# Moving the final output store of a decode kernel from SyncE to ScalarE

## The chip, the cores and the metric

The kernel runs on one core of a Trainium2 chip. The metric is the device time of one execution in microseconds (us). "Time" below is always that figure. "Span" is what the trace covers, from the first to the last recorded instruction; it is somewhat shorter than the time.

Names: PE is the matrix engine, DVE the vector engine, ACT or ScalarE the activation engine, POOL or GpSimd the general one, SP or SyncE the engine that here only synchronises and issues transfers. "SPq" and "ACTq" are the instruction sequencers of SyncE and ScalarE. A semaphore is a counter on which an engine can wait; a transfer increments one as it completes, and its landing is the last of these increments. DVE's last operation converts the result to bf16 in the tile `fin_bf`; it is called the cast below.

## The reference

One decode step: layer norm of a single row, attention of 32 query heads over 8 K/V heads with 65,536 cached positions each, an output projection, and a small feed-forward network in parallel.

```python
xn = _layernorm(x)                               # x is [1, 1, 512]
# attention: q = xn @ wq; k_cache, v_cache are [1, 8, 65536, 128] in bf16
o  = softmax(q k^T / sqrt(128)) v                # 32 heads, 4 per K/V head
return x + o @ wo + (gelu(xn @ w1 + b1) @ w2 + b2)   # [1, 1, 512], bf16
```

The two caches are 134 MB each, so the step is mostly a matter of reading about 280 MB once. The output is 512 bf16 numbers, 1 KB.

## The kernel before

A small scheduler in the program records operations for each engine with what they read and write, and derives the semaphore waits. SyncE issues every large load. The operations before the last few are emitted in a block, at whose end all engines meet at a barrier; the rest is emitted after it. This is the end of the program, the only part that the change touches:

```python
    rest = {}
    for i, (g0, n) in enumerate(WP):
        if i == 1:                                   # from here on: after the block
            rest.update((e, len(e.ops)) for e in (PE, DVE, SP))
        for r in range(g0 * HPG, (g0 + n) * HPG):
            for kt in range(KT):
                fin_mm(kt, oX_bf[:, r:r + 1], wo_sb[:, r, kt * 128:(kt + 1) * 128], ...)
    ...                                              # the last head's matmuls
    NR = 32 * (KT - 1) + 1
    sch.op(DVE, lambda: dve.tensor_copy(out=fin_bf[0:NR, :], in_=pR[0:NR, 0:128]),
           reads=[f"pss{R}"], writes=["fin"])
    ev_out = sch.dma(
        SP,
        lambda: sp.dma_start(out=out[0, 0].rearrange("(kt p) -> kt p", p=128), in_=fin_bf[0:NR:32, :]),
        sem_out, reads=["fin"], writes=["out_dram"],
    )
    ...
    with nc.Block() as block:
        ...                                          # gpsimd: _emit(e, POOL.ops)
        @block.sync
        def _(e):
            _emit(e, SP.ops[:rest[SP]])
        @block.scalar
        def _(e):
            _emit_rolled(e, ACT.ops, [m[1] for m in marks2])
        ...                                          # vector, tensor
    for e, obj in ((PE, pe), (DVE, dve), (SP, sp)):
        _emit(obj, e.ops[rest[e]:])
    sp.wait_ge(ev_out.sem, ev_out.val)
```

The four parts of the result stand in partitions 0, 32, 64 and 96, so the store moves four rows of 256 bytes.

## Time and profile before

| | before |
|---|---|
| time, median of 3 runs | 656.82 us (656.76 to 657.03) |
| span of the profiled run | 655.5 us |
| last weight rows landed, by the chain of waits | 652.7 us |
| end of the cast of the result, `fin_bf` | 653.79 us |
| last instruction (SyncE, landing of the store) | 655.49 us |

First, lines of the page of the profiled run of before: the span; the busy share of the DMA engines in 40 equal slices, in tenths (9 is 90% or more); two of the DMA queues with their packets, megabytes and share of the 16 engines' time; the HBM traffic; and the chain of work that ended last, by engine.

```profile
span 655.5 us, 27968 instructions
...
DMA  9999999999999999999999999999999999999997
...
q1 hardware_dynamic: 8616, 280.50, 99.4%
...
q10 hardware_dynamic: 148, 0.01, 0.0%
...
HBM read 280.50 MB, written 0.00 MB: 428 GB/s over the span
...
DMA 63%; PE 34%; issue 2%; DVE 0%; SPq 0%
```

The DMA engines are busy for 90% or more of all slices but the last (70%), and the chain lies in DMA and PE: the kernel is a stream of loads with PE close behind it. Queue 1 is SyncE's; queue 10 is ScalarE's, with 148 packets from three small loads at the start.

The timeline of before near its end has, per row, start and duration in us, engine, line of the kernel, operation, output and input, and in brackets the idle time before it with what ended it:

```profile
652.82 0.36 PEld L805 LDWEIGHTS pss<-kv,oT_all 128*1 128x1 bf16 x16 [0.76 <-issue]
652.85 0.60 PE L805 MATMUL pss<-kv,oT_all 128*1 128x128 bf16 x16 [0.50 <-DMA kv<-in_A_wo_dram]
653.50 0.29 DVE L823 CAST fin_bf<-pss 97x128 bf16<-97x128 f32 x1 [4.78 <-PE pss L805]
653.82 0.64 SPq L827 DMA_DIRECT2D out_dram<-fin_bf  x1
```

And the waits of SyncE in before: waiter, what it waited for, total us, times, longest.

```profile
SPq L842 <- PEq L842: 13.8, 1, 13.8
...
SPq L827 <- DVE fin_bf L823: 3.4, 1, 3.4
SPq L866 <- DMA out_dram<-fin_bf: 1.0, 1, 1.0
```

The last load, in the chain of before and then in that of after (start and duration in us):

```profile
635.59 17.13 DMA kv<-in_A_wo_dram
```

SyncE stands at the block's barrier for 13.8 us, then waits 3.4 us for the cast, issues the store, and waits 1.0 us for it to land. The engine that issues the store is never late.

### The profile page before, as it was taken

How to read it: one execution, taken by the hardware profiler on the slowest of the kernel's cores; microseconds unless marked ns; L12 is line 12 of the kernel's file. 1: busy time of each engine (PE TensorE's matmuls, PEld its weight loads, DVE VectorE, ACT ScalarE, POOL GpSimd, SP SyncE). 2: the span in 40 equal slices, each digit the busy share in tenths (PEclk: the TensorE clock that was granted, in tenths of full speed). 3: DMA queues.
4: the chain of work that ended last, by engine and by line, in shares of the span. 5: the costliest groups of instructions: out<-in, count | busy, mean ns of one | idle time of the engine just before them, and what ended most of it. 6: DMA issues, size and time to landing. Idle time of an engine off the chain costs nothing.

```text
span 655.5 us, 27968 instructions
## 1 busy us (share of the span) xinstructions
PE 536.8 (82%) x12682; PEld 509.6 (78%) x12682; DVE 275.8 (42%) x574; ACT 245.0 (37%) x454; POOL 2.9 (0%) x27
## 2 busy tenths in 40 slices
PE   2478699989789697878969788896978879797897
PEld 0277598979788696878959687895978879697886
DVE  3244072625436171453516245261534516154353
ACT  0134162634425162352506235160443516145251
POOL 0000000000000000000000000000000000000000
PEclk9788596967869596786959679595886959578695
DMA  9999999999999999999999999999999999999997
GB/s 386 445 431 422 431 430 432 446 422 450 416 448 420 428 460 404 436 428 454 430 420 440 426 442 422 426 460 408 444 426 450 430 418 436 428 460 404 432 432 305
DMA packets 8774, 280.65 MB, mean 428 GB/s; under 512 B 1082, under 2 KB 1596, under 8 KB 1724
## 3 DMA queue, kind: packets, MB, share of 16 engines
q1 hardware_dynamic: 8616, 280.50, 99.4%
q8 instruction: 8, 0.13, 0.1%
q10 hardware_dynamic: 148, 0.01, 0.0%
q14 instruction: 2, 0.02, 0.0%
HBM read 280.50 MB, written 0.00 MB: 428 GB/s over the span
## 4 chain that ended last, share of the span: by engine, by line
DMA 63%; PE 34%; issue 2%; DVE 0%; SPq 0%
DMA kv<-in_A_k_cache_dram 61%; PE pst L590 27%; PE pss L610 4%; DMA kv<-in_A_wo_dram 3%; PE pO L681 2%; PE pA L637 0%; PE pA L648 0%; DVE pmax L618 0%; PE pA L697 0%; PE pss L805 0%; DVE gmax L639 0%; DVE diag L641 0%; SPq L470 0%; SPq L467 0%; DVE fin_bf L823 0%
## 5 line engine op out<-in xcount | busy, mean ns | idle before, releaser
L600 ACT ACTIVATE kt_ring<-pst 128x1024 bf16<-128x1024 bf16 x192 | 195.6, 1027 | 310.6 <-PE pst L590 309.2
L590 PE MATMUL pst<-ident_bf,kv 128*128 128x128 bf16 x4096 | 281.8, 235 | 34.5 <-DMA kv<-in_A_k_cache_dram 34.4
L590 PEld LDWEIGHTS pst<-ident_bf,kv 128*128 128x128 bf16 x4096 | 263.5, 107 | 42.8 <-DMA kv<-in_A_k_cache_dram 35.9
L598 DVE COPY kt_ring<-pst 128x1024 bf16<-128x1024 bf16 x320 | 210.7, 687 | 119.1 <-PE pst L590 116.9
L681 PE MATMUL pO<-P_bf,kv 128*128 128x4 bf16 x4096 | 115.1, 166 | 37.6 <-DMA kv<-in_A_v_cache_dram 31.2
L681 PEld LDWEIGHTS pO<-P_bf,kv 128*128 128x128 bf16 x4096 | 113.6, 104 | 38.9 <-DMA kv<-in_A_v_cache_dram 32.2
L610 PE MATMUL pss<-q_cur,kt_ring 128*128 128x4 bf16 x4096 | 111.9, 164 | 5.1 <-issue 5.1
L610 PEld LDWEIGHTS pss<-q_cur,kt_ring 128*128 128x128 bf16 x4096 | 109.3, 96 | 5.3 <-issue 5.3
L659 ACT ACTIVATE P_bf<-pss,negm 128x128 bf16<-128x128 f32 x128 | 50.9, 548 | 67.4 <-DVE negm L651 67.4
L690 DVE COPY o_all<-pO 128x4 f32 (+1 forms) x32 | 5.2, 162 | 120.7 <-PE pO L681 119.9
L618 DVE TENSOR_REDUCE pmax<-pss 128x4 f32<-128x512 f32 x32 | 22.1, 692 | 69.0 <-PE pss L610 69.0
L659 ACT ACTIVATION_READ_ACCUMULATOR P_bf<-pss,negm 128x1 f32 x128 | 35.4, 277 | 0.0
L648 PEld LDWEIGHTS pA<-diag,ones_f 4*128 4x128 f32 x64 | 12.6, 244 | 18.1 <-DVE diag L641 16.5
L637 PE MATMUL pA<-ident_f,pmax 128*4 128x128 f32 x64 | 14.2, 310 | 12.6 <-DVE pmax L618 12.6
L648 PE MATMUL pA<-diag,ones_f 4*128 4x4 f32 x64 | 15.4, 309 | 10.0 <-DVE diag L641 10.0
L637 PEld LDWEIGHTS pA<-ident_f,pmax 128*4 128x4 f32 x64 | 2.9, 84 | 15.7 <-DVE pmax L618 14.0
L639 DVE TENSOR_REDUCE gmax<-pA 4x1 f32<-4x128 f32 x32 | 8.8, 274 | 9.4 <-PE pA L637 9.4
L673 DVE COPY sums_all<-sums 128x8 f32 (+1 forms) x16 | 2.7, 172 | 23.4 <-ACT P_bf L659 23.4
L697 PE MATMUL pA<-sums_all,ones_f 128*128 128x128 f32 x32 | 12.4, 491 | 0.0
L518 PE MATMUL pA<-ones_bf,xn_row 1*128 1x1 bf16 x4 | 0.3, 172 | 12.7 <-DVE xn_row L514 12.7
L518 PEld LDWEIGHTS pA<-ones_bf,xn_row 1*128 1x128 bf16 x4 | 0.2, 115 | 12.7 <-DVE xn_row L514 12.7
L651 DVE TENSOR_SCALAR negm<-pA 128x4 f32<-128x4 f32 x32 | 5.1, 161 | 10.8 <-PE pA L648 10.8
(78 smaller groups left out, 63.8 us busy)
## 6 DMA issues: line engine op xcount, KB each, us to landing
kv<-in_A_k_cache_dram SPq DMA_DIRECT2D x32, 4096.0 KB, 27.5
kv<-in_A_v_cache_dram SPq DMA_DIRECT2D x4, 4096.0 KB, 23.1
kv<-in_A_wq_dram SPq DMA_DIRECT2D x1, 4096.0 KB, 12.3
kv<-in_B_w_dram SPq DMA_DIRECT2D x2, 1792.0 KB, 17.8
kv<-in_A_wo_dram SPq DMA_DIRECT2D x1, 2048.0 KB, 23.7
kv<-in_A_wo_dram SPq DMA_DIRECT2D x1, 1024.0 KB, 25.9
kv<-in_A_wo_dram SPq DMA_DIRECT2D x1, 512.0 KB, 26.6
kv<-in_A_wo_dram SPq DMA_DIRECT2D x1, 384.0 KB, 17.1
```

The lines of the kernel that those rows point to most:

```text
L590: lambda tb=tb, at=at, b=b, tt=s * TPB + t: pe.transpose(pst[tb][:, at * 128:(at + 1) * 128], slot[b][:, tt, :], ident_bf[:, :]),
L598: e, fn = DVE, lambda tb=tb, dst=dst: dve.tensor_copy(out=dst, in_=pst[tb][:, :])
L600: e, fn = ACT, lambda tb=tb, dst=dst: act.activation(out=dst, in_=pst[tb][:, :], func=ACTF.Copy)
L610: lambda k=k, kb=kb, at=at, t=t: pe.matmul(pss[k][:, at:at + HPG], lhsT=kt_ring[:, kb * BCOL + t * 128:kb * BCOL + (t + 1) * 128], rhs=q_c ...
L618: lambda k=k: dve.tensor_reduce(out=pmax[:, :], in_=pss[k][:, 0:CW].rearrange("p (t j) -> p j t", j=HPG), axis=AX.X, op=ALU.max),
L637: sch.op(PE, lambda: pe.matmul(pA[0:HPG, PA_ST:PA_ST + 128], lhsT=pmax[:, 0:HPG], rhs=ident_f[:, :], start=True, stop=True), reads=["pmax" ...
L639: sch.op(DVE, lambda: dve.tensor_reduce(out=gmax4[:, :], in_=pA[0:HPG, PA_ST:PA_ST + 128], axis=AX.X, op=ALU.max), reads=["pA"], writes=[" ...
L648: sch.op(PE, lambda: pe.matmul(pA[:, PA_SB:PA_SB + HPG], lhsT=ones_f[0:HPG, 0:128], rhs=diag4[0:HPG, 0:HPG], start=True, stop=True), reads ...
L659: lambda k=k, at=at, j=j, src=src: act.activation(out=P_v[k][:, :, j], in_=src[:, :, j], func=ACTF.Exp, bias=negm[:, at:at + 1], scale=1.0 ...
L681: lambda k=k, t=t: pe.matmul(pO[:, 0:HPG], lhsT=vslot[:, k * TPD + t, :], rhs=P_v[k][:, t, :], start=t == 0, stop=t == TPD - 1),
L690: sch.op(DVE, lambda: dve.tensor_copy(out=o_all[:, at_pair(i, PW, k * HPG, HPG)], in_=pO[:, 0:HPG]), reads=["pO"], writes=[f"o{k}"])
L697: sch.op(PE, lambda: pe.matmul(pA[:, PA_SUM:PA_SUM + NC], lhsT=ones_f[:, :], rhs=sums_all[:, :], start=True, stop=True), reads=["ones_f", ...
```

## The change

The store and the wait for its landing move from SyncE to ScalarE, whose own work has ended by then. SyncE's program then ends at the block's barrier.

```diff
-            rest.update((e, len(e.ops)) for e in (PE, DVE, SP))
+            rest.update((e, len(e.ops)) for e in (PE, DVE, ACT))
...
     ev_out = sch.dma(
-        SP,
-        lambda: sp.dma_start(out=out[0, 0].rearrange("(kt p) -> kt p", p=128), in_=fin_bf[0:NR:32, :]),
+        ACT,
+        lambda: act.dma_start(out=out[0, 0].rearrange("(kt p) -> kt p", p=128), in_=fin_bf[0:NR:32, :]),
         sem_out, reads=["fin"], writes=["out_dram"],
     )
...
-            _emit(e, SP.ops[:rest[SP]])
+            _emit(e, SP.ops)
...
-            _emit_rolled(e, ACT.ops, [m[1] for m in marks2])
+            _emit_rolled(e, ACT.ops[:rest[ACT]], [m[1] for m in marks2])
...
-    for e, obj in ((PE, pe), (DVE, dve), (SP, sp)):
+    for e, obj in ((PE, pe), (DVE, dve), (ACT, act)):
         _emit(obj, e.ops[rest[e]:])
-    sp.wait_ge(ev_out.sem, ev_out.val)
+    act.wait_ge(ev_out.sem, ev_out.val)
```

## The prediction

> **What bounds the kernel now.** One core; the span is 655.5 us, the time 656.82 us. The page's DMA queue table shows 280.50 MB read at a mean of 428 GB/s, and the DMA row of the slices is at 9 tenths or more in 39 of 40 slices. The chain of waits is 63% DMA (61% K cache loads), 34% PE, and under 1% everything else. The kernel is a stream of loads with the transposes just behind it. The change touches only the end.
>
> **The end, as the timeline and the waits show it.** The last weight rows land at about 652.7 us. PE does the last 16 output matmuls (652.85, 0.62 us), DVE casts the result into `fin_bf` (653.50, 0.29 us), SyncE starts the output store at 653.82 (issue 0.64 us, to 654.46), then waits 1.0 us for its landing, and its last instruction at 655.5 ends the span. So the part that the change can alter is 1.67 us, 0.25% of the span: issue 0.64 plus landing about 1.04. All of it is on the critical path.
>
> **What the change removes, adds and moves.** It removes one wait, one DMA issue and one landing wait from SyncE and puts the same three on ScalarE. Nothing is saved by overlap: SyncE's list of issues shows nothing after 636.0, so the store was not queued behind anything, and ScalarE is not busy either (last activation ends at 642.4, its drain ends before the block's barrier at 650.4, which PE's drain decides). Loops and loads stay as they are. The wait for DVE took about 0.03 us between cast and issue; I expect the same on ScalarE.
>
> **Costs.** Issue: ScalarE's three issues at the start took 0.52, 0.21 and 0.39 us; the 0.52 was its first. SyncE's loads took 0.33 us at the median, up to 0.56 back to back, and the store 0.64. So the 0.64 of the store looks like a cold cost (other tensor, four rows only) that ScalarE will also pay: estimate 0.5 to 0.7 us. Landing: the Trainium skill, "DMA: Bandwidth & Descriptors", section "Issuing engines are not separate DMA queues", says that DMAs run on the same 16 DMA engines whoever starts them. This trace agrees as far as it goes: nothing else is moving after 652.7, so the 1.04 us of issue end to landing should stay, give or take 0.1. ScalarE's queue has been idle since the first microseconds; if an idle queue starts slowly, a few tenths more.
>
> Sum: -0.15 to +0.3 us on the path, centre +0.03.
>
> **Prediction.** 656.85 us, range 656.2 to 657.5, which is mostly run-to-run and chip-to-chip spread (three runs of before lie within 0.27 us). Faster by over 2%: 0.005. Within 2%: 0.99. Slower by over 2%: 0.005.
>
> **What would show it right or wrong.**
> - Everything up to the cast of `fin_bf` (about 653.5) is at the same time within a few tenths; DMA share and 428 GB/s unchanged.
> - The store's issue appears on ScalarE's queue about 0.03 us after the cast, takes 0.5 to 0.7 us, and lands about 1.0 us after that; SyncE's last instruction is the block's barrier near 650.4.
>
> **What would make it wrong.** A slow start of ScalarE's long-idle queue, or ScalarE not having the last instructions fetched after its loop (either would show as a gap between cast and issue, or between issue and landing). Or a fixed cost at the program's end that depends on which engine ends last: time less span is now 1.3 us and the trace does not show what is in it.

## More of the kernel before

```profile
634.82 17.97 DMA kv<-in_A_wo_dram
```

It landed at 652.72 in before and at 652.79 in after, about 0.8 us ahead of the cast in both, so nothing of the load stream is left on the queue when the store is due.

From the end of the cast to the end of the span it is 1.70 us, 0.26% of the span.

## The result, and the profile after

| | before | after |
|---|---|---|
| time, median | 656.88 us (the 3 runs above and a fourth) | 656.99 us (4 runs, 656.89 to 657.19) |
| ratio after to before | | 1.0002, 95% interval 0.9985 to 1.0019 |
| span of the profiled run | 655.49 us | 655.60 us |
| end of cast to start of issue | 0.028 us | 0.031 us |
| issue of the store | 0.637 us | 0.616 us |
| start of issue to first packet | 1.230 us | 1.257 us |
| end of cast to last increment of the store's semaphore | 1.668 us | 1.700 us |
| end of cast to end of span | 1.702 us | 1.738 us |

The ratios and intervals here are not quite the ratios of the medians. The finer lines of the table come from the single records of the trace (instructions, packets, semaphore increments), which have nanoseconds where the timeline rounds.

The lines of the page of after that answer to those of before:

```profile
span 655.6 us, 27968 instructions
...
DMA  9999999999999999999999999999999999999997
...
q1 hardware_dynamic: 8608, 280.50, 99.4%
...
q10 hardware_dynamic: 156, 0.01, 0.0%
...
HBM read 280.50 MB, written 0.00 MB: 428 GB/s over the span
...
DMA 64%; PE 33%; issue 2%; DVE 0%; SPq 0%
```

Exactly eight packets (four of data, four of semaphore increments) have moved from queue 1 to queue 10. Everything else of the stream is the same. The end of the timeline of after:

```profile
652.90 0.35 PEld L805 LDWEIGHTS pss<-kv,oT_all 128*1 128x1 bf16 x16 [0.73 <-issue]
652.93 0.60 PE L805 MATMUL pss<-kv,oT_all 128*1 128x128 bf16 x16 [0.47 <-DMA kv<-in_A_wo_dram]
653.58 0.29 DVE L823 CAST fin_bf<-pss 97x128 bf16<-97x128 f32 x1 [5.48 <-PE pss L805]
653.90 0.62 ACTq L827 DMA_DIRECT2D out_dram<-fin_bf  x1
```

In the waits of SyncE in after, the store's two lines are gone and the barrier is left:

```profile
SPq L842 <- PEq L842: 14.4, 1, 14.4
```

Note how little of the store is in the row of its issue. The Trainium skill, "Perfetto Trace Analysis", section "DMA Instruction — HWDGE (DVE, Sync)", says that the recorded duration of such an instruction ends with the sequencer's part and leaves the movement of data out. The trace agrees: the row of before ends at 654.46, its first packet of data starts at 655.05 and its last increment comes at 655.46. Whoever costs a store by the row alone misses 1.0 us out of 1.67.

### The profile page after: what moved, and what is told of

Same layout as the page of the kernel before. It is cut to its first block, busy times and chain, and to the rows that moved or that the text cites. A ratio compares the mean times of both kernels' runs of the same rounds, so it can differ in the third digit from the quotient of the medians.

```text
span 655.6 us, 27968 instructions
## 1 busy us (share of the span) xinstructions
PE 535.2 (82%) x12682; PEld 507.1 (77%) x12682; DVE 275.3 (42%) x574; ACT 245.2 (37%) x454; POOL 2.9 (0%) x27
## 4 chain that ended last, share of the span: by engine, by line
DMA 64%; PE 33%; issue 2%; DVE 0%; SPq 0%
DMA kv<-in_A_k_cache_dram 61%; PE pst L590 26%; PE pss L610 4%; DMA kv<-in_A_wo_dram 3%; PE pO L681 2%; PE pA L637 0%; PE pA L648 0%; DVE pmax L618 0%; PE pA L697 0%; PE pss L805 0%; DVE gmax L639 0%; DVE diag L641 0%; SPq L470 0%; SPq L467 0%; DVE fin_bf L823 0%
```

## Experiments

The theories:

- **A.** The store is three pieces in series (issue, transfer, landing), all on the critical path, and ScalarE does them at the cost that SyncE had. Nothing is gained as nothing waited for SyncE.
- **B.** There is a cost at the program's end, outside the trace, that depends on which engine ends last.
- **C.** ScalarE's queue is itself slower, long idle or cold as it is.
- **D.** The end of the program is hidden behind something else, so that no change to the store could be seen.

The first four runs shared one chip and nine runs of before (median 656.73 us, 656.67 to 657.01).

### 1. The changed kernel again, in five rounds

No edit. Expected:

> The changed kernel once more, timed in five rounds. Theory A (the same three pieces, issue, transfer, landing, done by another engine at the same cost): ratio within 0.05% of 1, that is within 0.3 us. Rival B (a cost at the program's end that depends on which engine ends last): time less span was 1.31 us in the profiled run of before and 1.45 to 1.6 us in the four runs of the changed kernel; B expects the changed kernel 0.1 to 0.25 us slower at an equal span, in every round. Rival C (ScalarE's queue itself is slower): issue start to last instruction in the trace longer than the 1.67 us of before by over 0.1 us.

Measured: 657.04 us median, ratio 1.0006 (0.9992 to 1.0019). The mean time is 657.13 us against 656.78, 0.35 us more. Of that, 0.18 us is span (655.60 against 655.42; the spans of before alone range from 655.2 to 655.7), and 0.17 us is time less span: 1.53 us on the average (1.47 to 1.58) against 1.36 (1.28 to 1.47). From cast to end of span it took 1.735 us, 0.03 more than in before. So C is no more than 0.03 us in this trace; B is as expected on the average (the two ranges of time less span touch at 1.47); A's mark of 0.05% was just missed, at 0.06% with an interval that holds 1.

### 2. One half of the change: SyncE issues, ScalarE waits

```diff
 # on the kernel before
-    sp.wait_ge(ev_out.sem, ev_out.val)
+    act.wait_ge(ev_out.sem, ev_out.val)
```

> Half of the change: SyncE issues the store as before, ScalarE alone waits for its landing and ends last. A: as before within 0.3 us. B: 0.1 to 0.25 us slower than before, as the changed kernel is. C: as before. In the trace the store on SyncE's queue takes about 0.64 us and lands about 1.0 us later in all theories.

Measured: 656.87 us, ratio 1.0003 (0.999 to 1.0017). Time less span 1.51 us (1.47 to 1.54). Issue 0.637 us; cast to end of span 1.712 us. The store is that of before, and the end cost is that of the changed kernel.

### 3. The other half: ScalarE issues, SyncE waits

```diff
 # on the kernel after
-    act.wait_ge(ev_out.sem, ev_out.val)
+    sp.wait_ge(ev_out.sem, ev_out.val)
```

> The other half: ScalarE issues the store, SyncE alone waits for its landing and ends last. A: as before within 0.3 us. B: as before (SyncE ends last). C: slower than before by what ScalarE's queue costs more.

Measured: 656.85 us, ratio 1.0001 (0.9987 to 1.0015). Time less span 1.37 us (1.31 to 1.46). Issue 0.612 us; cast to end of span 1.729 us. The store is that of the changed kernel, and the end cost is that of before. Runs 2 and 3 together show that the extra 0.15 us outside the trace goes with the engine that *waits last*, not with the one that issues.

### 4. The store done twice

```diff
 # on the kernel after, following the first store
+    sch.wait_ev(ACT, ev_out)
+    ev_out = sch.dma(
+        ACT,
+        lambda: act.dma_start(out=out[0, 0].rearrange("(kt p) -> kt p", p=128), in_=fin_bf[0:NR:32, :]),
+        sem_out, reads=["fin"], writes=["out_dram"],
+    )
```

> The changed kernel with the store done a second time after the first has landed. If the store's issue and landing lie in full on the critical path (A), the time grows by one whole issue and landing, 1.3 to 1.7 us, 0.2 to 0.26%. Rival D (the tail of the program is hidden behind something the trace does not show, so that no change of the store could be seen in the time): under 0.3 us. If the 0.62 us of the first issue is a cost of the first use of this tensor or direction on this queue, the second issue takes 0.2 to 0.35 us; if every such store costs it, 0.6 us again.

Measured: 658.49 us, ratio to before 1.0026 (1.0012 to 1.004). Against the changed kernel of run 1 the mean grew by 1.42 us (658.55 against 657.13), and from cast to end of span it takes 3.327 us in place of 1.735, 1.59 us more. The 0.17 us between the two figures is of the size by which the spans of one kernel vary. So the store is on the critical path in full, and D falls: had the change cost or saved a microsecond, it would have been seen. The timeline of this kernel, columns as above:

```profile
653.98 0.61 ACTq L827 DMA_DIRECT2D out_dram<-fin_bf  x1
655.67 0.53 ACTq L833 DMA_DIRECT2D out_dram<-fin_bf  x1
```

The second issue, right behind the first on the same queue and to the same tensor, takes 0.53 us. I had expected 0.2 to 0.35, or 0.6; it is nearer the second, so first use explains only 0.09 us.

### 5 and 6. An early store to warm the queue

```diff
 # on the kernel after (ScalarE), and the same on the kernel before with SyncE
+    sch.op(DVE, lambda: dve.memset(fin_bf[:, :], 0.0), writes=["fin"])
+    ev_warm = sch.dma(
+        ACT,
+        lambda: act.dma_start(out=out[0, 0].rearrange("(kt p) -> kt p", p=128), in_=fin_bf[0:97:32, :]),
+        sem_out, reads=["fin"], writes=["out_dram"],
+    )
     DVE.pending = ACT.pending = 64
```

With ScalarE:

> The changed kernel with an early store of zeros into the same output by ScalarE, near the start; the real store waits for it (long landed by then). If the 0.62 us issue is a cost of first use on this queue, and lasts, the final issue falls to 0.2 to 0.35 us and the end comes 0.3 to 0.4 us earlier after the cast; if it comes from the queue's 640 us of idling, or belongs to every such store, it stays at about 0.6 us. The time moves by under 0.5 us in each case.

With SyncE:

> The kernel before with the same early store by SyncE. SyncE's queue never idles for long here, so idling predicts nothing for it; first use predicts a final issue of 0.3 us in place of 0.64; a cost of every such store predicts 0.64 again.

Measured, beside seven runs of before (656.93 us): 656.84 us with ScalarE (ratio 0.9999, 0.9982 to 1.0016) and 656.67 us with SyncE (0.9996, 0.9979 to 1.0012). The final issue, in the two kernels in turn (duration in ns: least, median, most):

```profile
L833 ACTq DMA_DIRECT2D out_dram<-fin_bf x1: 548/548/548, 653.7 to 653.7; - x1
```

```profile
L833 SPq DMA_DIRECT2D out_dram<-fin_bf x1: 536/536/536, 653.8 to 653.8; - x1
```

It fell from 616 to 548 ns and from 637 to 536 ns. I had expected 0.2 to 0.35 us if it were a cost of first use, so that reading is wrong for the most part: 0.07 to 0.10 us is first use, and the other 0.53 to 0.55 us belongs to each such store on either engine. (The early stores themselves, near 3.2 us, took 0.606 us on ScalarE and 0.640 on SyncE to issue, like the unwarmed ones at the end.) ScalarE's 650 us of idling cost little: the issue here (548 ns) and the second one of run 4 (525 ns), whose queue had just been used, differ by 0.02 us. From cast to end of span it took 1.665 us with ScalarE (1.735 in run 1) and 1.631 with SyncE (1.702). The warmed SyncE version is thus, by the trace, 0.07 us shorter at its end than the kernel before; the timing cannot confirm so little, since its interval holds 1.

### 7. GpSimd as the issuer

```diff
 # on the kernel after (and POOL in place of ACT in rest, in the block, behind it and in the final wait)
-        ACT,
-        lambda: act.dma_start(...
+        POOL,
+        lambda: pool.dma_start(...
```

> The store is issued and waited for by GpSimd, the third way to issue one. Theory A in its strong form (who issues does not matter) expects the same time within 0.3 us. The weaker form (SyncE and ScalarE have the same kind of issue, GpSimd another) expects it later: the Trainium skill, DMA: Bandwidth & Descriptors, Specifications, gives a first byte of about 1 us for this path against 0.6 for the other; my estimate is 0.4 to 1.5 us longer from cast to last instruction.

Measured: 657.64 us, ratio 1.0011 (0.9995 to 1.0028); the means differ by 0.74 us (657.65 against 656.92, before rounding). The timeline:

```profile
653.28 0.29 DVE L823 CAST fin_bf<-pss 97x128 bf16<-97x128 f32 x1 [5.20 <-PE pss L805]
653.87 0.67 POOL L827 DMA_DIRECT2D out_dram<-fin_bf  x1 [10.71 <-DVE fin_bf L823]
```

From the end of the cast to the start of the issue 0.295 us pass (0.03 on SyncE and ScalarE), and from cast to end of span 2.068 us, 0.37 more than in before; my lower bound was 0.4. Time less span is 1.93 us (1.86 to 2.02) against 1.39 in the runs of before beside it, a further 0.54 us outside the trace. So A does not hold for every issuer: SyncE and ScalarE are alike, GpSimd is not. A later first byte, as cited, is seen when it is counted from the moment that the store waits for: from the end of the cast to the first data packet 1.54 us pass, 0.28 more than on SyncE (1.26), where the two figures cited differ by 0.4. Counted from the end of the issue's row it does not show (0.57 us against SyncE's 0.59), so the delay falls into the 0.295 us ahead of the row; the times of rows on POOL are rough, and whether GpSimd was already at work then is not shown. A further 0.08 us of the 0.37 lies between the first packet and the last increment, of which this trace has 16 and that of before 5. The rest of the cost is the 0.54 us outside the trace. The mean spans differ by 0.20 us only, as the part ahead of the cast varies from run to run.

### 8 and 9. A load in flight on SyncE's queue

```diff
 # on the kernel before, just ahead of the store; SyncE waits for it at the end
+    ev_dum = sch.dma(
+        SP,
+        lambda: sp.dma_start(out=slot[3], in_=A_k_cache[0, 0, 0:CKEYS, :].rearrange("(p t) d -> p t d", p=128)),
+        sem_dum, reads=[f"pss{R}"], writes=["vb"],
+    )
 # the second kernel: the same on the kernel after, so the load on SyncE and the store on ScalarE
 # (left out here: the declaration of sem_dum, the waits at the end, SP in rest and in the block)
```

Both on SyncE:

> The kernel before with a useless 4 MB load issued by SyncE once the last matmul is done, just ahead of the store, and waited for at the end. If a queue serves its transfers in order, the store, behind the load on SyncE's queue, lands only near the load's end, about 10 us after its issue; if the engines mix transfers of one queue, it lands within 2 to 3 us. The time is about 10 us longer either way (the load, an estimate from 428 GB/s), so the trace decides: issue to landing of the store.

Load on SyncE, store on ScalarE:

> The same useless load on SyncE's queue, the store on ScalarE's. The two queues share the 16 engines but take turns: the store should land 1.5 to 5 us after its issue, well before the load's end. If the queue does not matter at all, it lands as in the twin with both on SyncE. This is the case in which the change would be worth something.

Measured: 667.05 and 666.96 us (two runs each; before 656.80). The timelines of the two, in turn:

```profile
653.63 0.33 SPq L828 DMA_DIRECT2D kv<-in_A_k_cache_dram  x1
653.64 0.29 DVE L824 CAST fin_bf<-pss 97x128 bf16<-97x128 f32 x1 [4.62 <-PE pss L806]
654.01 0.65 SPq L833 DMA_DIRECT2D out_dram<-fin_bf  x1
```

```profile
653.29 0.33 SPq L828 DMA_DIRECT2D kv<-in_A_k_cache_dram  x1
653.30 0.29 DVE L824 CAST fin_bf<-pss 97x128 bf16<-97x128 f32 x1 [4.72 <-PE pss L806]
653.62 0.62 ACTq L833 DMA_DIRECT2D out_dram<-fin_bf  x1
```

When the store's data went, from the trace's records of packets and semaphore increments (us from the span's start):

```
                    issue starts   first data packet (256 B)   last increment   load's last increment
both on SyncE       654.01         664.89                      665.63           665.70
store on ScalarE    653.62         658.64                      660.43           665.58
```

Behind a load on its own queue, the store waits for nearly the whole load: 11.6 us from issue to landing, in place of 1.64 (the table above: 1.668 less 0.028). On the other engine's queue it lands after 6.8 us, 5.2 us ahead of the load's end, but not promptly: I had expected 1.5 to 5 us. The Trainium skill, "DMA: Bandwidth & Descriptors", section "Queues, rings and completion order", says that each DMA engine consumes one ring in order and takes turns between the rings of different queues, a whole packet at a time. Both traces agree with that. A turn can be read from the second: each of the store's four increment packets starts 1.22 us after its packet of data (658.64 and 659.86 for the first; in the kernel after it is 0.01 us), which is the time of one 32 KB piece of the load (1.21 us in the records). The first packet of data, 4.4 us after the end of the issue, came when three rounds of such pieces had gone (started at about 654.3, 656.2 and 657.4); why it had no turn after the first is not shown. The time of the kernel hardly differs between the two (667.05 and 666.96 us), as the load is waited for in both: only the store lands earlier. The change can be worth something where the store's landing is what is waited for last and its queue still holds other transfers. The original kernel does not have that: its last load has landed before the cast.

### 10 and 11. ScalarE busy when the store is due

```diff
 # on the kernel after, ahead of the store: run 10
+    for _ in range(6):
+        sch.op(ACT, lambda: act.activation(out=kt_ring[:, 0:1024], in_=pst[0][:, :], func=ACTF.Copy),
+               reads=["pst0"], writes=["kt0_0"])
 # run 11: six different destinations, kt_ring[:, n * 1024:(n + 1) * 1024], so that no copy waits for another
```

Run 10:

> The changed kernel with six useless ScalarE copies of 1.03 us each (6.2 us, an estimate from the mean of those in the loop) between the block's barrier and the store, so that ScalarE computes from about 650.4 to 656.6 while the store is due at 653.9. If ScalarE's instructions are strictly one after another, the store is issued after 656 and the time grows by 2 to 3.5 us; if its sequencer can issue a DMA while the compute part is busy, the store is issued at about 654 and the time grows by at most 1 us (the copies end at 656.6).

Run 11:

> As act_busy, but the six copies go to six different places, so that none waits for the one before it (there each waited for its predecessor's end, and the store could not be issued before the fifth copy had ended, whatever the sequencer can do). If ScalarE's sequencer runs ahead of its compute part to the DMA, the store is issued while several copies are still to come, at about 653.9, and the end of the span is set by the copies at about 656.6. If it starts each copy only when the one before has ended, the store is issued at about 655.4 again, just after the sixth copy's start, and the time is 1.5 to 2 us longer than before, as in act_busy.

Measured: 658.65 us in run 10 (before 656.80) and 657.50 us in run 11 (before 656.88), two runs each. ScalarE's rows in the two, in turn:

```profile
650.12 6.30 ACT L826 ACTIVATE kt_ring<-pst 128x1024 bf16<-128x1024 bf16 x6 [8.22 <-PEq L845]
655.40 0.62 ACTq L830 DMA_DIRECT2D out_dram<-fin_bf  x1
```

```profile
650.38 3.77 ACT L826 ACTIVATE kt_ring<-pst 128x1024 bf16<-128x1024 bf16 x4 [8.16 <-PEq L845]
653.68 0.62 ACTq L830 DMA_DIRECT2D out_dram<-fin_bf  x1
654.00 1.98 ACT L826 ACTIVATE kt_ring<-pst 128x1024 bf16<-128x1024 bf16 x2
```

In run 10 neither of my two numbers came: each copy had a semaphore wait for the one before it, so the store stood behind the wait of the sixth and was issued 6 ns after that copy's start, 1.9 us after the cast. The span shows that a store on ScalarE can be late by ScalarE's own waits. In run 11, where no copy waits, the store was issued 0.031 us after the cast, as if ScalarE were idle, and two copies that stand *ahead* of it in the program started after it. The Trainium skill, "Perfetto Trace Analysis", section "DVE / Act Engine Instruction (TENSOR_ADD, Activation, etc)", describes a queue between sequencer and compute part, into which an instruction moves once its semaphores are satisfied; run 11 agrees. The end of run 11 (2.33 us after the cast) is set by the last copy, at 656.0 rather than at the expected 656.6, as these copies started 0.90 us apart.

### The difference outside the trace, over all timed runs

Time less span, the means of the runs of each kernel:

| ends last | kernels | time less span |
|---|---|---|
| SyncE | before on four chips; 3; 6; 8; 9 | 1.36, 1.39, 1.34, 1.33; 1.37; 1.32; 1.35; 1.31 us |
| ScalarE | after; 1; 2; 4; 5; 10; 11 | 1.52; 1.53; 1.51; 1.49; 1.51; 1.50; 1.55 us |
| GpSimd | 7 | 1.93 us |

Kernel 9 is of use here: ScalarE issues the store and waits for it, but SyncE ends last, and the difference is SyncE's 1.31. Spans of the timed runs are kept to 0.1 us, so a single difference is good to 0.05 us and only the means are compared. What makes up this difference is not in any trace here. The Trainium skill, "Runtime: NRT & Kernel Launch", section "The ~15µs preamble/postamble breakdown", lists a barrier that waits for all engines after the kernel; that its cost depends on who comes last would fit, but no run here shows it.

## Why the prediction was right

The predicted 656.85 us, with a range of 656.2 to 657.5, met 656.99 us. The range is 1.3 us wide and "no effect at all" lies in it too, so that meeting it says little; what the record supports is the account of the parts. Point by point:

- *"All of it is on the critical path."* Shown by run 4: a second store costs 1.59 us in the trace.
- *"Nothing is saved by overlap."* Right: SyncE had waited 3.4 us for the cast. Runs 8 and 9 show what the opposite case looks like.
- *The wait for DVE, about 0.03 us.* 0.031 us.
- *Issue 0.5 to 0.7 us.* 0.616 us, but partly for the wrong reason. "Looks like a cold cost" holds for 0.07 to 0.10 us of it (runs 4 to 6); the rest is paid by every such store. Why a four-row store takes 0.53 us to issue, where a 4 MB load takes 0.33, was not tested; ScalarE's second load at the start, one row of 1 KB, took 0.21, so neither few bytes nor few rows alone explain it.
- *Issue end to landing stays at 1.04 us, give or take 0.1.* To the last increment it was 1.00 us before and 1.05 after. The section "Issuing engines are not separate DMA queues", cited in the prediction, agrees for an idle machine. Runs 8 and 9 show the limit of it: the engines are shared, but the place in the queue is not.
- *"Sum: -0.15 to +0.3 us on the path, centre +0.03."* Cast to end of span grew by 0.036 us in the profiled pair.
- *What would make it wrong: "a fixed cost at the program's end that depends on which engine ends last".* This one exists, at 0.15 us (runs 1 to 3). It was named as a risk and not put into the sum. It is the largest part of the change's effect that was shown, and still small against the range.
- *A slow start of a long-idle queue.* Not found: 0.02 us between runs 4 and 5.

The rest of the 0.35 us in run 1, 0.15 us of span ahead of the cast, is within what the spans of one kernel vary from run to run, and no cause is claimed for it.

## What to carry to other kernels

Moving a small transfer to another engine's queue gained nothing here, where the issuer was early and its queue empty. It can pay if the issuer is late (not tested) or its queue still holds other transfers (the landing in runs 8 and 9); read both from the waits of the issuer and from the landing of the last load ahead of the store, before making the change. A lone store at the end costs its issue plus about 1 us until its landing, whichever of SyncE and ScalarE issues it; what was seen to change that was an earlier store on the same queue (0.07 us less, in single traces) and one more store in series (1.59 us more). The engine that ends last is worth 0.15 us outside the trace. On a compute engine, check also what the engine's own instructions ahead of the store wait for.

## What the Trainium skill lacked or had wrong

- "Runtime: NRT & Kernel Launch": the page does not say that the time outside the kernel's instructions depends on which engine ends last. Here it was 1.31 to 1.39 us for SyncE, 1.49 to 1.55 for ScalarE and 1.93 for GpSimd.
- "DMA: Bandwidth & Descriptors", section "Issuing engines are not separate DMA queues": its heading and its advice read as if the issuer hardly mattered. With a 4 MB load in flight, the same store landed 11.6 us after its issue on the loaded queue and 6.8 us after it on the other (runs 8 and 9); the time of the whole kernel, which the load ended, was the same within 0.1 us, which the section's advice fits. The section on queues and rings of the same page does cover this.
- The same page, section "Specifications", gives first bytes of about 0.6 us (SyncE, ScalarE) and 1 us (GpSimd). It does not say from when. From the end of the issue it was 0.59 (SyncE), 0.64 (ScalarE) and 0.57 us (GpSimd); from the end of the cast, which the store waits for, 1.26, 1.29 and 1.54 us. The page has nothing on the 0.54 us more that GpSimd cost outside the trace.
- I found on no page, as a time, what the issue of a store of few rows takes: 0.61 to 0.64 us at its first use, 0.53 to 0.55 us later, against 0.33 us for a 4 MB load on SyncE (the median of before's loads).
